# Attention and a mixture of experts on one core: where the next expert's operands are made

## The chip, the cores and the metric

The kernel runs on one core of a Trainium2 chip. TensorE multiplies matrices into PSUM (8 banks of 512 f32 a partition), VectorE (DVE) and ScalarE (ACT) read PSUM and SBUF, GpSimd (POOL) works on SBUF and issues gathers and scatters of rows, SyncE (SP) issues the other DMAs. Each engine executes its own instructions in the order in which they were written. The metric is the time of one execution on the device, in microseconds (us); the median of several runs counts.

## The reference, cut to what matters

Attention over 4 batches, 8 heads, 768 positions gives 3072 rows of 512 numbers, x. Each row goes to two of eight experts:

```
for e in range(8):
    for k in range(2):
        mask = top2[:, k] == e
        h = np.maximum(x[mask] @ w1[e], 0.0)              # 512 -> 1024
        out[mask] += top2_w[mask, k, None] * (h @ w2[e])  # 1024 -> 512
```

Everything is f32. The kernel gets near f32 from f16 matmuls: each operand is split into hi = f16(a) and lo = f16(a - hi), and a product is hi*hi + lo*hi + hi*lo.

## The kernel before, in words

Attention fills the first 140 us and is not touched. Then the experts follow, sorted by size: 816, 832, 816, 800, 784, 768, 768, 768 rows at most. Experts 0 and 1 use a plain product. For experts e = 2 to 7 the product x @ w1 is made of **seven half-size products** instead of eight (as Strassen and Winograd do): x and w1 are cut in quarters, and sums of quarters are operands too. These sums, and the hi and lo parts of all operands, must be made for the next expert while the current one computes.

**The seven stage.** For each of four column groups i = 0 to 3 the products u = 1 to 7 are written by `seven(e, i, u)`; below (i,u) names one. Each is six matmuls (`prod`, line 1338) with half of the rows as columns. (i,1) and (i,2) are accumulated in a bank called b1, (i,3) and (i,5) in b5, (i,4), (i,6), (i,7) in b2; b2 and b5 have two banks each, for even and odd i. b1 is og[:, i % 2]: the two halves of one tile `o` of two banks. After (i,1) ScalarE copies b1 into b2 (line 1357), after (i,5) b5 into SBUF (line 1360); after (i,6) VectorE adds into b5 (line 1362), after (i,7) into c22 (line 1364). Four of the seven, u = 2, 3, 4, 7, end with `hi()` on ScalarE (relu to f16, line 1368) and `lo()` on VectorE (line 1371), which write the hidden rows `hth` and `htl`. TensorE's order: (0,1) (0,5) at the end of the expert before (`seven_head`); (0,2) (0,6); then blocks (i,1) (i,5) (i-1,7) (i,2) (i,6) (i-1,3) (i-1,4) for i = 1 to 3; last (3,7), a part of the first chunk's second product, (3,3), (3,4).

**The second stage.** h @ w2 in chunks of 128 rows, 24 matmuls each (line 1405; line 1402 for the last, shorter chunk of a large expert). A chunk is accumulated in a PSUM tile `pt` (two buffers), `mm2_out` (line 912, VectorE) scales it by the gate and adds the rows read earlier from the output (`prev`, a POOL gather), and POOL scatters the row sum back. Experts with up to 768 rows have 6 chunks, larger ones 7. Ahead of the last chunk stands `seven_head` of the next expert, which needs that expert's w1 part 0 and all its tokens.

**What is woven in.** A plan written by hand puts each preparing step at a **hook**: hook t is called after a certain product (3 to 31) or after a third of a chunk (32 + 3c and on, for chunk c). What a hook calls is written on each engine's queue at that place. The steps for the next expert n:

- `w_load` (lines 731, 735): 512 KB of w1 (parts 0 to 3) or w2 (parts 4 to 7) into one of four buffers `stg`, on SP's queue. `w1_sums` (line 1318): four sums of quarters of 128x256 on POOL, into another `stg` buffer. `w1_hi` (ScalarE, line 1327) and `w1_lo` (VectorE, line 1331): two pieces each, 768 and 1024 columns.
- `w_hi`, `w_lo` (lines 740, 758): the w2 parts of expert e itself, during its seven stage, one operation of 1024 columns each.
- `xs_gather`: two row gathers on POOL (line 90) into one of two buffers `xg`, for token group g: 0 to 2 are full (2 x 128 rows), 3 holds the tail rows over 768 (experts 2, 3 and 4 only). `xs_sums` (lines 1272 to 1274): three VectorE operations. `xs_hi` (ScalarE, line 1291) and `xs_lo` (VectorE, line 1300): four pieces each, two for each of two parts. `xs_turn` (line 1307): transposing DMAs on SP's queue into the operand tiles.

The operand tiles are used again from stages that are over: an even expert's hi parts lie in XTE[0] and its lo parts in XTE[1], an odd one's hi parts in w2 tiles of expert 1 and its lo parts in `xl`. XTE[1] holds expert 1's own tokens, which its plain product (mm1, lines 851 to 860, hooks 0 to 15) reads to its end.

Of the kernel before, what the change touches and what calls it, by code (L numbers as in the profile page):

```python
# [8 lines left out]
F32 = mybir.dt.float32  # L9
F16 = mybir.dt.float16  # L10
# [53 lines left out]
def attn_moe(ctx, tc, qt, kt, vt, wgn, noise, w1, w2, out):  # L64
# [1154 lines left out]
            x.rearrange("p a b -> p (a b)")[:, :n]  # L1219

    def seven_init():
        G["xs"] = [[flat16(XTE[0], 14, 1), flat16(XTE[1], 14, 1)], [None, G["xl"]]]
        G["wp"] = [flat16(WT[i][n], 3584, 0).rearrange("p (l o x) -> p l o x", l=2, o=7)
                   for i in range(2) for n in ("w1h", "w1l")]

# [34 lines left out]
                     in_offset=bass.IndirectOffsetOnAxis(ap=ap, axis=0), bounds_check=N - 1, oob_is_err=False)  # L1260
        XR[n, g] = [x.rearrange("p s c -> p (s c)").bitcast(F32), -(-k // 16) * 16]

    def xs_sums(n, g):
        if (n, g) not in XR:
            return
        x, r = XR[n, g]
        t = [work.tile([P, DC, P], F32, name="xt", bufs=GN).rearrange("p a b -> p (a b)") for i in range(2)]
        XR[n, g] += [t[0], t[1]]
        ta, tb = [z[:r] for z in t]
        x = x[:r]  # L1270
        v = x.rearrange("p (a b c) -> p a b c", a=2, b=2)
        nc.vector.tensor_tensor(ta.rearrange("p (a c) -> p a c", a=2), v[:, 1], v[:, :, 0], op=OP.subtract)
        nc.vector.tensor_tensor(tb[:, :256], x[:, 768:], ta[:, :256], op=OP.subtract)
        nc.vector.tensor_tensor(tb[:, 256:], x[:, 256:512], tb[:, :256], op=OP.subtract)

    def xs_pieces(n, g, part):
        x, r, ta, tb = XR[n, g]
# [3 lines left out]

    XH = {}

    def xs_hi(n, g):
        if (n, g) not in XR:
            return
        for part in range(2):
            r, ps = xs_pieces(n, g, part)
            t = XH[n, g, part, 0] = work.tile([P, DM], F32, name="x", bufs=5).bitcast(F16)
            for c, k, src in ps:  # L1290
                nc.scalar.activation(t[:r, c:c + k], src, AF.Copy)  # L1291

    def xs_lo(n, g):
        if (n, g) not in XR:
            return
        for part in range(2):
            r, ps = xs_pieces(n, g, part)
            t = XH[n, g, part, 1] = work.tile([P, DM], F32, name="x", bufs=5).bitcast(F16)
            for c, k, src in ps:
                nc.vector.tensor_tensor(t[:r, c:c + k], src, XH[n, g, part, 0][:r, c:c + k], op=OP.subtract)  # L1300

    def xs_turn(n, g, lo):
        if (n, g) not in XR:
            return
        for part in range(2):
            r = XR[n, g][1]
            nc.sync.dma_start_transpose(out=xs_part(n, lo, part)[:, :, P * g:P * g + r],
                                        in_=XH[n, g, part, lo][:r, :NS_[part]])

    SS = {}  # L1310

    def w1_sums(n, f):
        t = SS[n, f] = stage.tile([P, SW], F32, name="stg")[:, :1024]
        a21, a11, a12, a22 = [SG[n, f][:, 256 * i:256 * i + 256] for i in range(4)]
        s1, s2, s3, s4 = [t[:, 256 * i:256 * i + 256] for i in range(4)]
        for o, x, y, op in ((s1, a21, a22, OP.add), (s2, s1, a11, OP.subtract), (s3, a11, a21, OP.subtract),
                            (s4, a12, s2, OP.subtract)):
            nc.gpsimd.tensor_tensor(o, x, y, op=op)  # L1318

    def w1_parts(n, f):  # L1320
        w = G["wp"][f]
        return [(s, w[:, 0, o].rearrange("p o x -> p (o x)"), w[:, 1, o].rearrange("p o x -> p (o x)"))
                for s, o in ((SG[n, f][:, 256:], slice(0, 3)), (SS[n, f], slice(3, 7)))]

    def w1_hi(n, f):
        for s, hi, lo in w1_parts(n, f):
            nc.scalar.activation(hi, s, AF.Copy, scale=W1S)

    def w1_lo(n, f):
        for s, hi, lo in w1_parts(n, f):  # L1330
            nc.vector.scalar_tensor_tensor(lo, s, W1S, hi, op0=OP.mult, op1=OP.subtract)  # L1331

    def prod(e, f, a, b, ph, start):
        k, w, h = 0, G["wp"][f], CAPS[e] // 2
# [12 lines left out]

    def seven(e, i, u):
        h = CAPS[e] // 2
        b1, b2, b5 = og[:, i % 2, :h], G["b2"][i % 2][:, :h], G["b5"][i % 2][:, :h]  # L1350
        hh, hl = HT
        f = i + (4 if u in (4, 7) else 0)
        t = slice(0, h) if u in (2, 4) else slice(h + tail(e), 2 * h + tail(e))
        a, b = ((0, 0), (1, 1), (6, 2), (2, 6), (3, 3), (4, 5), (5, 4))[u - 1]
        prod(e, i, a, b, {1: b1, 2: b1, 3: b5, 5: b5}.get(u, b2), u in (1, 5))
        if u == 1:
            nc.scalar.activation(b2, b1, AF.Copy)  # L1357
        elif u == 5:
            G["p5", i] = late[0].tile([P, XW], F32, name="p5", bufs=2)[:, :h]
            nc.scalar.activation(G["p5", i], b5, AF.Copy)  # L1360
        elif u == 6:
            nc.vector.tensor_tensor(b5, b2, G["p5", i], op=OP.add)  # L1362
        elif u == 7:
            nc.vector.tensor_tensor(G["c22"][:, :h], b2, G["p5", i], op=OP.add)
        src = {2: b1, 3: b5, 4: b2, 7: G["c22"][:, :h]}.get(u)

        def hi():
            nc.scalar.activation(hh[:, f, t], src, AF.Relu)  # L1368

        def lo():  # L1370
# [66 lines left out]
    def on(t, f, *a):  # L1437
        plan.setdefault(t, []).append((f, a))
# [2 lines left out]
        for f, a in plan.pop(t, []):  # L1441
            f(*a)

    def plan_w1(n, p, *t):
        for x, f in zip(t, (w_load, w1_sums, w1_hi, w1_lo)):
            on(x, f, n, p)

    def plan_x(n, g, *t):
        on(t[0], xs_gather, n, g)
        on(t[1], xs_sums, n, g)  # L1450
        on(t[2], xs_hi, n, g)
        on(t[2], xs_turn, n, g, 0)
        on(t[3], xs_lo, n, g)
        on(t[4], xs_turn, n, g, 1)

    def plan_late(n):
        plan_x(n, 1, 10, 34, 35, 36, 36)
        plan_x(n, 2, 26, 40, 41, 42, 42)
        plan_x(n, 3, 37, 44, 45, 46, 46)
        for i in range(4):  # L1460
            on((40, 40, 45, 45)[i], w_load, n, 4 + i)

    for e in range(1, E):
        pv = []
# [5 lines left out]
        n = e + 1  # L1470
        if e == 1:
            on(0, tail_ids)
            plan_w1(n, 0, 1, 4, 6, 7)
            plan_w1(n, 1, 3, 7, 9, 10)
            plan_w1(n, 2, 8, 11, 38, 39)
            plan_w1(n, 3, 11, 14, 43, 44)
            plan_x(n, 0, 8, 12, 13, 14, 32)
            plan_late(n)
        else:
            for i, (a, b) in enumerate(((3, 3), (4, 7), (8, 10), (11, 12))):  # L1480
                on(a, w_hi, e, 4 + i)
                on(b, w_lo, e, 4 + i)
            on(36, tail_next, e)
            if n < E:
                plan_w1(n, 0, 5, 9, 14, 17)
                plan_w1(n, 1, 13, 16, 32, 33)
                plan_w1(n, 2, 18, 24, 38, 39)
                plan_w1(n, 3, 34, 37, 43, 44)
                plan_x(n, 0, 6, 21, 22, 24, 25)
                plan_late(n)  # L1490
        for t in (17, 20, 23):
            on(t, prev)
        if e == 1:
# [171 lines left out]
```

## Time and profile before

| | |
|---|---|
| three runs | 691.88, 696.96, 700.48 us; median 696.96 |
| profiled execution | 703.5 us, its span in the trace 701.7 us |
| busy in the span | PE 641.4, DVE 451.7, POOL 321.1, ACT 313.4 us |
| expert 1's plain product | 208 to 242 us |
| seven stages | from 290 (expert 2), 361, 432, 501, 571, 637 us |
| second stages between them | 328 to 361, 399 to 432, 470 to 501, 539 to 571, 609 to 637, 668 to the end |

A row of the trace gives the start of an instruction in us from the span's start, its duration, engine, line, tiles written and read, and in brackets how long its engine sat idle before it and what ended that wait. Runs of like instructions are merged (x6), and consecutive instructions may overlap by some 0.1 to 0.2 us. Idle time counts where it delays the end; here that is the idle time of TensorE, which is busy nearly always.

### The profile page before, as it was taken

To read this page: it belongs to the slowest core of one execution; us is meant where nothing else is said; L and a number is where in the kernel's file an instruction comes from. 1 tells how busy PE (TensorE), PEld (TensorE's weight loads), DVE (VectorE), ACT (ScalarE), POOL (GpSimd) and SP (SyncE) were. 2 spreads that over 40 slices of the span, in tenths; PEclk is the share of its full clock that TensorE was granted. 3 is DMA by queue.
4 is the path that set the end of the run, shared out by engine and by line. 5 is a ranking of instruction groups with operands and counts; after the bars stand their busy time and mean duration, and the time that the engine had idled before them with its cause. 6 is when DMAs were issued, how large, how long until landed. Compare 5 with 4: busy or idle time off the path is not lost.

```text
span 701.7 us, 14247 instructions
## 1 busy us (share of the span) xinstructions
PE 641.4 (91%) x5343; PEld 368.1 (52%) x5343; DVE 451.7 (64%) x927; ACT 313.4 (45%) x688; POOL 321.1 (46%) x517
## 2 busy tenths in 40 slices
PE   8899989899999996888988998899989988999995
PEld 7677877655555542444454445444544444445542
DVE  5758988798863655378737774776377637765411
ACT  4777988731523431354334533453345234524300
POOL 4342242123256662294838483737383529353031
PEclk9999999999999999799999999999999999999998
DMA  9999999546493599347944694469546954692021
GB/s 298 314 301 310 320 276 316 206 149 202 148 208 102 134 167 238 110 126 155 245 144 135 153 243 136 138 153 217 187 129 150 226 162 130 150 276 94 1 88 47
DMA packets 123482, 127.81 MB, mean 182 GB/s; under 512 B 83084, under 2 KB 86484, under 8 KB 123404
## 3 DMA queue, kind: packets, MB, share of 16 engines
q1 hardware_dynamic: 111644, 90.54, 48.8%
q0 software_dynamic: 11760, 36.27, 18.1%
q8 instruction: 44, 0.72, 0.5%
q14 instruction: 34, 0.28, 0.1%
HBM read 82.03 MB, written 25.82 MB: 154 GB/s over the span
## 4 chain that ended last, share of the span: by engine, by line
PE 56%; DVE 13%; DMA 10%; issue 9%; ACT 6%; POOL 4%; SPq 2%; POOLq 0%; DVEq 0%; ACTq 0%
PE pt L1405 16%; PE h L851 9%; PE h L1338 7%; DMA xte<-x 5%; PE pt L902 4%; PE o L1338 4%; DVE htl L1371 3%; PE pt L341 2%; PE h L902 2%; PE s L318 2%; PE o L354 2%; DVE x L1300 2%; DVE w1h L1331 2%; ACT hth L1368 2%; DMA prev<-out_dram,tb 2%
## 5 line engine op out<-in xcount | busy, mean ns | idle before, releaser
L90 POOL DMA_INDIRECT out_dram<-y,tb x48 | 57.7, 1201 | 165.1 <-DVE y L912 147.0
L1318 POOL TENSOR_TENSOR stg<-stg 128x256 f32<-128x256 f32 x96 | 87.3, 929 | 32.5 <-DMA stg<-in_w_dram 18.9
L1405 PEld LDWEIGHTS <-hth 128*128 128x128 f16 x576 | 56.8, 99 | 67.8 <-issue 2.2
L90 POOL DMA_INDIRECT xg<-xd,tb x53 | 57.4, 1083 | 61.3 <-DVE dsc L653 31.4
L912 DVE SCALAR_TENSOR_TENSOR y<-pt,tb,prev 128x512 f32<-128x512 f32 x42 | 31.5, 750 | 83.7 <-PE pt L1405 72.5
L1338 PEld LDWEIGHTS <-w1l 128*128 128x128 f16 x504 | 50.9, 101 | 61.4 <-issue 29.5
L1338 PEld LDWEIGHTS <-w1h 128*128 128x128 f16 x504 | 49.4, 99 | 60.0 <-issue 23.1
L1405 PE MATMUL pt<-w2h,hth 128*128 128x512 f16 x288 | 70.1, 384 | 0.0
L1405 PE MATMUL pt<-w2l,hth 128*128 128x512 f16 x288 | 69.6, 381 | 0.0
L1405 PE MATMUL pt<-w2h,htl 128*128 128x512 f16 x288 | 69.0, 379 | 0.0
L1291 ACT ACTIVATE x<-xt 128x512 f16<-128x512 f32 (+2 forms) x42 | 25.6, 626 | 64.0 <-issue 51.7
L90 POOL DMA_INDIRECT prev<-out_dram,tb x42 | 47.6, 1133 | 12.4 <-issue 9.0
L333 ACT ACTIVATE p<-s,nm 128x120 f32<-128x120 f32 x192 | 51.1, 376 | 0.8
L851 PE MATMUL h<-xte,w1h 128*128 128x384 f16 (+2 forms) x248 | 49.4, 338 | 0.0
L1357 ACT ACTIVATE h<-o 128x384 f32<-128x384 f32 (+3 forms) x24 | 11.6, 482 | 80.7 <-PE o L1338 69.6
L1405 PEld LDWEIGHTS <-htl 128*128 128x128 f16 x288 | 28.2, 98 | 34.0
L1338 PE MATMUL h<-xte,w1h 128*128 128x408 f16 (+2 forms) x180 | 36.1, 344 | 5.0 <-DMA xte<-x 2.6
L1368 ACT ACTIVATE hth<-h 128x384 f16<-128x384 f32 (+3 forms) x48 | 23.9, 498 | 36.9 <-PE h L1338 36.5
L1338 PE MATMUL h<-xte,w1l 128*128 128x408 f16 (+2 forms) x180 | 35.8, 342 | 4.5 <-DVE h L1362 4.5
L857 ACT ACTIVATE hth<-h 128x384 f16<-128x384 f32 (+2 forms) x31 | 15.9, 514 | 47.4 <-PE h L851 47.1
L758 DVE SCALAR_TENSOR_TENSOR w2l<-stg,w2h 128x1024 f16<-128x1024 f32 x28 | 35.4, 1264 | 2.3 <-ACT w2h L740 2.3
L851 PEld LDWEIGHTS <-w1h 128*128 128x128 f16 x256 | 24.7, 98 | 19.5 <-issue 0.8
(286 smaller groups left out, 1314.5 us busy)
## 6 DMA issues: line engine op xcount, KB each, us to landing
stg<-in_w_dram SPq DMA_DIRECT2D x64, 512.0 KB
q<-in_qt_dram SPq DMA_DIRECT2D x24, 256.0 KB
xd<-x SPq DMA_DIRECT2D x24, 256.0 KB
out_dram<-xg SPq DMA_DIRECT2D x8, 768.0 KB
kb<-in_kt_dram SPq DMA_DIRECT2D x6, 768.0 KB
hth<-in_vt_dram SPq DMA_DIRECT2D x12, 260.0 KB
htl<-in_vt_dram SPq DMA_DIRECT2D x16, 195.0 KB
ve<-in_vt_dram SPq DMA_DIRECT2D x12, 260.0 KB
```

Source lines behind the costliest of these rows:

```text
L90: return nc.gpsimd.indirect_dma_start(**kw)
L333: nc.scalar.activation(PE_[t][:, a, hp, :], SC[t][:, a, hp, :], AF.Exp, bias=NM[t][:, 1, a, hp:hp + 1], scale=0.125)
L758: nc.vector.scalar_tensor_tensor(lo, SG[e, i], sc, hi, op0=OP.mult, op1=OP.subtract)
L851: nc.tensor.matmul(ph[:, :n], w1_of(w, wn, c, f), x[:, xo + c, c0:c1], start=(k == 0), stop=(k == 11))
L902: nc.tensor.matmul(py, hx[:, f, c * P:c * P + P], wv[:, f, :], start=st, stop=sp)
L912: nc.vector.scalar_tensor_tensor(y, py[:, :d], gw, pv[:, :d], op0=OP.mult, op1=OP.add)
L1291: nc.scalar.activation(t[:r, c:c + k], src, AF.Copy)
L1318: nc.gpsimd.tensor_tensor(o, x, y, op=op)
L1338: nc.tensor.matmul(ph[:, :h], w[:, la, a, P * j:P * j + P], x[:, j, :h], start=start and k == 0, stop=k == 5, skip_group_check=True)
L1368: nc.scalar.activation(hh[:, f, t], src, AF.Relu)
L1371: nc.vector.scalar_tensor_tensor(hl[:, f, t], src, 0.0, hh[:, f, t], op0=OP.max, op1=OP.subtract)
L1405: nc.tensor.matmul(py, x, wv[:, f, :], start=st, stop=sp, skip_group_check=True)
```

## The change

Four things. The sums of w1 quarters go from POOL to VectorE. The preparing steps are cut into single operations, each with a hook of its own, and the hooks are set anew: the next expert's token groups 0 and 1 are made in the seven stage, group 2, the tail and all four w1 parts in the second stage (for expert 2: groups 0 to 2 and w1 parts 0 and 1 during expert 1's plain product); w2 parts 6 and 7 are loaded at hook 4 of their own expert. For odd i, b1 is a `pt` tile in place of the second half of `o`. XTE[1] and `xl` change roles, so expert 2's lo parts lie in `xl`.

```diff
     def seven_init():
-        G["xs"] = [[flat16(XTE[0], 14, 1), flat16(XTE[1], 14, 1)], [None, G["xl"]]]
+        G["xs"] = [[flat16(XTE[0], 14, 1), G["xl"]], [None, flat16(XTE[1], 14, 1)]]
...
+    def xs_lo(n, g, part, i):
...
+        c, k, src = ps[i]
+        nc.vector.tensor_tensor(XH[n, g, part, 1][:r, c:c + k], src, XH[n, g, part, 0][:r, c:c + k], op=OP.subtract)
+        if i == 1:
+            xs_turn(n, g, part, 1)
...
         for o, x, y, op in ((s1, a21, a22, OP.add), (s2, s1, a11, OP.subtract), (s3, a11, a21, OP.subtract),
                             (s4, a12, s2, OP.subtract)):
-            nc.gpsimd.tensor_tensor(o, x, y, op=op)
+            nc.vector.tensor_tensor(o, x, y, op=op)
...
     def seven(e, i, u):
         h = CAPS[e] // 2
-        b1, b2, b5 = og[:, i % 2, :h], G["b2"][i % 2][:, :h], G["b5"][i % 2][:, :h]
+        if u == 1:
+            G["b1", i] = psum.tile([P, 512], F32, name="pt", bufs=2) if i % 2 else og[:, 0]
+        b1, b2, b5 = G["b1", i][:, :h], G["b2"][i % 2][:, :h], G["b5"][i % 2][:, :h]
...
+    def plan_w1(n, p, t, *u):
+        on(t, w_load, n, p)
+        on(u[0], w1_sums, n, p)
+        for i in range(2):
+            on(u[1 + i], w1_hi, n, p, i)
+        for i in range(2):
+            on(u[3 + i], w1_lo, n, p, i)
+
+    def plan_x(n, g, t, s, h, l):
+        on(t, xs_gather, n, g)
+        for i in range(3):
+            on(s[i], xs_sums, n, g, i)
+        for i in range(2):
+            on(h[i], xs_hi, n, g, i)
         for i in range(4):
-            on((40, 40, 45, 45)[i], w_load, n, 4 + i)
+            on(l[i], xs_lo, n, g, i // 2, i % 2)
...
         if e == 1:
             on(0, tail_ids)
-            plan_w1(n, 0, 1, 4, 6, 7)
-            plan_w1(n, 1, 3, 7, 9, 10)
-            plan_w1(n, 2, 8, 11, 38, 39)
-            plan_w1(n, 3, 11, 14, 43, 44)
-            plan_x(n, 0, 8, 12, 13, 14, 32)
-            plan_late(n)
+            plan_x(n, 0, 0, (3, 3, 3), (4, 4), (5, 5, 5, 5))
+            plan_x(n, 1, 1, (6, 6, 6), (7, 7), (8, 8, 8, 8))
+            plan_w1(n, 0, 1, 9, 9, 10, 10, 10)
+            plan_w1(n, 1, 2, 11, 11, 12, 12, 12)
+            plan_x(n, 2, 7, (13, 13, 13), (14, 14), (15, 15, 15, 15))
+            plan_w1(n, 2, 11, 33, 33, 34, 34, 34)
+            plan_x(n, 3, 12, (35, 35, 35), (36, 36), (37, 37, 37, 37))
+            plan_w1(n, 3, 13, 38, 38, 39, 39, 39)
         else:
-            for i, (a, b) in enumerate(((3, 3), (4, 7), (8, 10), (11, 12))):
+            for i, (a, b) in enumerate(((3, 4), (4, 7), (8, 14), (15, 21))):
                 on(a, w_hi, e, 4 + i)
                 on(b, w_lo, e, 4 + i)
             on(36, tail_next, e)
             if n < E:
-                plan_w1(n, 0, 5, 9, 14, 17)
-                plan_w1(n, 1, 13, 16, 32, 33)
-                plan_w1(n, 2, 18, 24, 38, 39)
-                plan_w1(n, 3, 34, 37, 43, 44)
-                plan_x(n, 0, 6, 21, 22, 24, 25)
-                plan_late(n)
+                plan_x(n, 0, 3, (9, 11, 12), (10, 13), (15, 16, 18, 19))
+                plan_x(n, 1, 5, (22, 23, 25), (24, 27), (28, 29, 29, 31))
+                plan_w1(n, 0, 8, 32, 32, 33, 33, 34)
+                plan_w1(n, 1, 15, 35, 35, 36, 36, 37)
+                plan_x(n, 2, 20, (38, 38, 38), (39, 39), (40, 40, 40, 40))
+                plan_w1(n, 2, 35, 41, 41, 42, 42, 43)
+                plan_x(n, 3, 32, (44, 44, 44), (45, 45), (46, 46, 46, 46))
+                plan_w1(n, 3, 38, 47, 47, 48, 48, 49)
+            if e > 2:
+                on(4, w_load, e, 6)
+                on(4, w_load, e, 7)
+        if n < E:
+            on(44, w_load, n, 4)
+            on(44, w_load, n, 5)
+        if e == 1:
+            on(48, w_load, n, 6)
+            on(48, w_load, n, 7)
```

Before, `plan_w1(n, p, load, sums, hi, lo)` and `plan_x(n, g, gather, sums, hi, lo, turn of lo)` had one hook for each whole step, and `plan_late` had groups 1, 2 and 3 at (10, 34, 35, 36, 36), (26, 40, 41, 42, 42), (37, 44, 45, 46, 46).

## Rows read from the trace of the kernel before

**Rows 1.** The page, costliest groups: busy us, mean ns of one, idle before it.

```profile
L1318 POOL TENSOR_TENSOR stg<-stg 128x256 f32<-128x256 f32 x96 | 87.3, 929 | 32.5 <-DMA stg<-in_w_dram 18.9
```

**Rows 2.** Stretches: length, then each engine's busy time, granted clock, DMA share, GB/s.

```profile
208.00:242.00 34.00, 34.00 (x197) 18.90 (x194) 17.31 (x26) 12.73 (x23) 20.08 (x31) 1.00 0.38 112
432.00:470.00 38.00, 33.27 (x183) 18.02 (x180) 26.77 (x40) 20.15 (x36) 22.42 (x32) 0.96 0.46 129
470.00:501.00 31.00, 31.00 (x183) 15.51 (x181) 16.75 (x25) 7.67 (x12) 16.42 (x26) 1.00 0.98 221
```

**Rows 3.** TensorE's waits, 242 to 702 us: total us, how many, longest.

```profile
PE o L1338 <- DVE htl L1371: 12.9, 11, 2.5
PE o L1338 <- DMA xte<-x: 11.4, 3, 5.9
PE h L1338 <- DVE h L1362: 7.5, 5, 2.1
PE h L1338 <- DVE htl L1371: 4.0, 6, 0.9
PE h L1338 <- DMA xte<-x: 2.6, 1, 2.6
PE o L1338 <- DMA xl<-x: 1.8, 1, 1.8
```

**Rows 4.** TensorE in order of time, expert 4's seven products: start, duration, idle before.

```profile
432.11 1.17 PE L1338 MATMUL o<-xte,w1h 128*128 128x392 f16 x6
...
447.53 2.15 PE L1338 MATMUL h<-xte,w1l 128*128 128x392 f16 x12
452.06 1.84 PE L1338 MATMUL o<-xte,w1l 128*128 128x392 f16 x6 [2.37 <-DVE htl L1371]
453.69 2.17 PE L1338 MATMUL h<-xte,w1l 128*128 128x392 f16 x6
```

**Rows 5.** VectorE in order of time, expert 4, both stages.

```profile
447.92 3.14 DVE L1331 SCALAR_TENSOR_TENSOR w1h<-stg,w1h 128x768 f16<-128x768 f32 x2
...
451.45 0.55 DVE L1371 SCALAR_TENSOR_TENSOR htl<-o,hth 128x392 f16<-128x392 f32 x1
...
452.87 0.68 DVE L1272 TENSOR_TENSOR xt<-xg 128x512 f32<-128x512 f32 x1
453.58 0.42 DVE L1273 TENSOR_TENSOR xt<-xg,xt 128x256 f32<-128x256 f32 x1
...
460.42 1.28 DVE L1300 TENSOR_TENSOR x<-xt,x 128x512 f16<-128x512 f32 x2
...
475.78 0.75 DVE L912 SCALAR_TENSOR_TENSOR y<-pt,tb,prev 128x512 f32<-128x512 f32 x1 [0.60 <-PE pt L1405]
476.45 2.08 DVE L1331 SCALAR_TENSOR_TENSOR w1h<-stg,w1h 128x768 f16<-128x768 f32 x2
480.96 0.75 DVE L912 SCALAR_TENSOR_TENSOR y<-pt,tb,prev 128x512 f32<-128x512 f32 x1 [2.43 <-PE pt L1405]
```

**Rows 6.** POOL in order of time, expert 4's seven products.

```profile
435.62 1.29 POOL L90 DMA_INDIRECT xg<-xd,tb  x1 [0.22 <-issue]
...
447.52 4.80 POOL L1318 TENSOR_TENSOR stg<-stg 128x256 f32<-128x256 f32 x4
```

**Rows 7.** All engines, near 155 and 250 us: two gathers and their first readers.

```profile
153.20 1.01 POOL L90 DMA_INDIRECT xg<-xd,tb  x1 [20.06 <-DVE dsc L653]
...
156.66 0.63 ACT L809 ACTIVATE x<-xg 128x512 f16<-128x512 f32 x1 [2.34 <-DMA xg<-xd,tb]
...
244.46 1.00 POOL L90 DMA_INDIRECT xg<-xd,tb  x1 [0.22 <-issue]
...
255.02 0.63 ACT L1291 ACTIVATE x<-xg 128x512 f16<-128x512 f32 x1 [2.43 <-DMA xg<-xd,tb]
```

**Rows 8.** The chain that ended last, 340 to 360 us: start, us, what.

```profile
350.51 1.68 DVE x L1300 x4
...
352.44 4.47 DMA xl<-x
```

More of the change, by code (lines that the diff above doesn't have):

```diff
@@ L1261, in xs_gather, with xs_sums @@
         XR[n, g] = [x.rearrange("p s c -> p (s c)").bitcast(F32), -(-k // 16) * 16]
-    def xs_sums(n, g):
+    def xs_sums(n, g, k):
         if (n, g) not in XR:
             return
[L1266 to L1270, printed above, removed]
-        v = x.rearrange("p (a b c) -> p a b c", a=2, b=2)
-        nc.vector.tensor_tensor(ta.rearrange("p (a c) -> p a c", a=2), v[:, 1], v[:, :, 0], op=OP.subtract)
-        nc.vector.tensor_tensor(tb[:, :256], x[:, 768:], ta[:, :256], op=OP.subtract)
-        nc.vector.tensor_tensor(tb[:, 256:], x[:, 256:512], tb[:, :256], op=OP.subtract)
+        if k == 0:
+            XR[n, g] += [work.tile([P, DC, P], F32, name="xt", bufs=GN).rearrange("p a b -> p (a b)")
+                         for i in range(2)]
+        x, r, ta, tb = XR[n, g]
+        x, ta, tb = x[:r], ta[:r], tb[:r]
+        v = x.rearrange("p (a b c) -> p a b c", a=2, b=2)
+        if k == 0:
+            nc.vector.tensor_tensor(ta.rearrange("p (a c) -> p a c", a=2), v[:, 1], v[:, :, 0], op=OP.subtract)
+        elif k == 1:
+            nc.vector.tensor_tensor(tb[:, :256], x[:, 768:], ta[:, :256], op=OP.subtract)
+        else:
+            nc.vector.tensor_tensor(tb[:, 256:], x[:, 256:512], tb[:, :256], op=OP.subtract)
     def xs_pieces(n, g, part):
@@ L1282, in attn_moe, with xs_hi, xs_turn @@
     XH = {}
-    def xs_hi(n, g):
+    def xs_hi(n, g, part):
         if (n, g) not in XR:
             return
[L1287 to L1293, printed above, removed]
+        r, ps = xs_pieces(n, g, part)
+        t = XH[n, g, part, 0] = work.tile([P, DM], F32, name="x", bufs=5).bitcast(F16)
+        for c, k, src in ps:
+            nc.scalar.activation(t[:r, c:c + k], src, AF.Copy)
+        xs_turn(n, g, part, 0)
+    def xs_lo(n, g, part, i):
         if (n, g) not in XR:
             return
[L1296 to L1308, printed above, removed]
+        r, ps = xs_pieces(n, g, part)
+        if i == 0:
+            XH[n, g, part, 1] = work.tile([P, DM], F32, name="x", bufs=5).bitcast(F16)
+        c, k, src = ps[i]
+        nc.vector.tensor_tensor(XH[n, g, part, 1][:r, c:c + k], src, XH[n, g, part, 0][:r, c:c + k], op=OP.subtract)
+        if i == 1:
+            xs_turn(n, g, part, 1)
+    def xs_turn(n, g, part, lo):
+        r = XR[n, g][1]
+        nc.sync.dma_start_transpose(out=xs_part(n, lo, part)[:, :, P * g:P * g + r],
+                                    in_=XH[n, g, part, lo][:r, :NS_[part]])
     SS = {}
@@ L1322, in w1_parts, with w1_hi, w1_lo @@
         return [(s, w[:, 0, o].rearrange("p o x -> p (o x)"), w[:, 1, o].rearrange("p o x -> p (o x)"))
[L1323 to L1331, printed above, removed]
+                for s, o in ((SG[n, f][:, 256:], slice(0, 3)), (SS.get((n, f)), slice(3, 7))) if s is not None]
+    def w1_hi(n, f, i):
+        x, hi, lo = w1_parts(n, f)[i]
+        nc.scalar.activation(hi, x, AF.Copy, scale=W1S)
+    def w1_lo(n, f, i):
+        x, hi, lo = w1_parts(n, f)[i]
+        nc.vector.scalar_tensor_tensor(lo, x, W1S, hi, op0=OP.mult, op1=OP.subtract)
     def prod(e, f, a, b, ph, start):
@@ L1442, in hook @@
             f(*a)
[L1444 to L1459, printed above, removed]
+    def plan_w1(n, p, t, *u):
[11 more added lines that the diff above has]
+            on(h[i], xs_hi, n, g, i)
         for i in range(4):
-            on((40, 40, 45, 45)[i], w_load, n, 4 + i)
+            on(l[i], xs_lo, n, g, i // 2, i % 2)
     for e in range(1, E):
```

## The prediction

> **What bounds the kernel now.** I read the page first for what the removed work costs: 87.3 us on POOL [rows 1]. It says nothing of the end yet. The view by stretches does: TensorE is busy nearly always, so only time in which it stands still or runs slowly can be won. From 470 to 501 (a second stage) it is busy all the time, from 432 to 470 (a seven stage) only 33.27 of 38.00 us [rows 2]. The table of who waited for whom, for TensorE alone from 242 us on, splits that idle time: 12.9 us in 11 waits of products into `o` on a VectorE `htl`, 4.0 us in 6 waits of products into `h` on `htl`, 7.5 us in 5 waits on line 1362, and 11.4 + 2.6 + 1.8 us in 5 waits on transposing DMAs [rows 3]. Together 40.2 us; all of it lies at the seven products or at the first two products of an expert, which the change rearranges.
>
> The wait into `o` is the largest. Expert 4 shows the pattern: product (3,1) starts at 452.06 after 2.37 us of idling, when the lo of (2,2), at 451.45 for 0.55 us, has ended [rows 4, 5]. Product (3,1) writes og[:,1]; that lo reads og[:,0]. So it is waiting for the neighbour bank in the same tile, not for its own. The lo was late because two lo operations of a weight piece (447.92, 3.14 us) stood ahead of it on VectorE [rows 5]. Then the clock: this product and the next take 1.84 and 2.17 us where an undisturbed one (432.11) takes 1.17 [rows 4]; the granted clock fell to the 1.2 GHz level. The dip costs 1.84 + 2.17 - 2 x 1.17 = 1.7 us. Five experts have the wait (6 further waits into `o` are about 0.2 us); four of the five stages show a granted clock of 0.96 as [rows 2] does for expert 4, the first shows 1.00.
>
> The wait on line 1362 is of the same kind: (3,7) needs b2 after line 1362 of (3,6) has read it, and that stood behind four lo pieces of token operands, the last pair at 460.42 for 1.28 us [rows 5].
>
> **The change part by part.**
> *Own banks.* Odd i now write b1 into a `pt` tile. Products (1,1) and (3,1) no longer share a tile with the lo of (0,2) and (2,2); their slot was last used by a second-stage chunk whose row sum is long done. Removed: 12.9 us [rows 3] and four dips, 4 x 1.7 = 6.8 us.
> *Dealt singly.* Between two products VectorE now gets one piece (0.42 to 0.68 us, or a w2 lo) instead of 2 to 3 us at a time, and the weight pieces leave the seven stage. Line 1362 of (3,6) has only small pieces ahead. Removed: 7.5 us. The waits into `h` on `htl` are product (2,5) waiting for the lo of (0,3), which stands behind a w2 lo at hook 12; there stands now one sum of 0.42 us. Removed: 4.0 us, but see the gather below.
> *Token operands early, XTE[1] and xl swapped.* Expert 2's lo parts no longer need XTE[1], which expert 1's first product still reads; its three full groups are made during that product. The 11.4 us are two waits at that first boundary (9.5 us) and one at the boundary into expert 4; the other two stand at those into experts 3 and 6, whose last transposes are late. Removed: 11.4 + 2.6 + 1.8 = 15.8 us.
> Sum removed: 12.9 + 6.8 + 7.5 + 4.0 + 15.8 = 47.0 us.
>
> *Weight sums from POOL to VectorE.* The 96 operations leave POOL [rows 1], where nothing on the path to the end depended on their speed except through row gathers behind them. On VectorE the nearest operation is a 128x256 subtraction, 0.42 us; four make 1.75 us a piece, 7.0 us an expert. Something comes back: beside a POOL sum (four took 4.80 us from 447.52) the pair of weight lo operations took 3.14 us, with POOL not summing 2.08 us [rows 5, 6]. VectorE's load per expert: the seven stage has 26.77 us now; two weight pieces leave (3.14 and about 2.1), one token group comes: sums of 0.68, 0.42 and 0.42, and lo pieces of 1.28 for one pair and, by its columns, three quarters of that for the other, 3.8 in all [rows 5], so about 25 us of 33 that remain. The second stage has 16.75; minus 3.8, plus two pieces at 2.1, plus 7.0, makes 24 of 31. Row sums come every 5.2 us (475.78 and 480.96) and take 0.75 [rows 5]; a chunk then holds 1.75 + 2.08 + 0.75 = 4.6 us, so a row sum is late by less than the 4.4 us that two `pt` buffers allow. I cost it at zero; if this cover were gone, see the second rival.
> *Expert 1's first product.* TensorE is busy 34.00 of 34.00 us with VectorE at 17.31 [rows 2]. Added: two more token groups (2 x 3.8) and two weight sums (2 x 1.75), 11 us, to about 28 of 34. Three spare banks of 2 us each cover a lag of 2 us around hooks 8 to 13. I take 0.5 us, between 0 and 2.
> *Queues.* SP issues the same loads and transposes in another order; four transposes and two w2 loads leave the second stage, where the DMA share is 0.98, for the seven stage, where it is 0.46 [rows 2]. POOL only loses work, so row gathers start no later.
>
> *What comes back.* (1) Token group 0 is gathered at hook 3 and summed at hook 9. POOL cannot start it before the scatter of the previous expert: expert 4 has its second half issued at 435.62 for 1.29 us, until 436.91 [rows 6], and nothing ahead of it changes. A gather landed 156.66 - 154.21 = 2.45 us after its issue ended when DMA was quiet [rows 7], so at 439.4. (2,5) is due ten products after 432.11, each about 1.0 us (two take 2.15 less one overlap of 0.17, from 447.53 [rows 4]), so at 442.1. Ahead of it on VectorE stand the three sums, lo of (0,7), line 1362, lo of (1,2) and lo of (0,3): 1.6 + 4 x 0.5 = 3.6 us. So the sums should start at 438.5; they are 0.9 us late, and everything behind them on VectorE with them. Five experts have it: 4.5 us (bounds 0 and 40, first rival).
> (2) Experts 3 and 4 have tail rows whose lo still comes at hook 46, behind the row sum of the fifth chunk. Before, these four took 1.68 us from 350.51 and the transpose another 4.47 [rows 8], while the product starts 5.2 us after that chunk. Each transpose now goes out after its own two pieces: 1.0 us of the 1.8 stays, 2.0 us for both. Experts 6 and 7 have group 2 at hook 40 and start at hook 47, two chunks or 10.4 us for a row sum (0.75), the lo (2.2) and two transposes: 0.5 each, 1.0 us.
> (3) In the block of i = 2 the lo of (1,3) must end before (3,5), 8 products or 7.9 us after the block begins. VectorE starts on it about 1.4 us late, with a w2 lo (1.1, the larger of the 2.08 pair), four lo pieces (2.2) and five of its own operations (5 x 0.55) ahead: 7.5, and small gaps between. I take 0.2 us five times, 1.0 us.
> Back: 4.5 + 2.0 + 1.0 + 1.0 + 0.5 = 9.0 us. Net 47.0 - 9.0 = 38.0 us. The profiled execution took 703.5 us (span 701.7), 6.5 above the median, so it would become 665.5 and the median 696.96 - 38.0 = **659 us**.
>
> **Rivals.**
> *The gather decides, and the kernel becomes slower.* Sums at hook 9 hold VectorE in order, hi pieces at hook 10 hold ScalarE. Each us by which the gather lands later than 2.45 is a us at (2,5), five times. Under a full DMA a gather that ended at 245.46 was used only at 255.02, 9.56 us later [rows 7]. With that, 5 x 8.0 = 40 us come back in place of 4.5, with five dips 8.5 more, so 659 + 35.5 + 8.5 = 703 us; it decides from a landing of about 8.4 us. For it: two more w2 loads are in flight there, and the w2 hi at hook 8 waits for one of them, too. Against: the seven stage has a DMA share of 0.46. A middle case, 4.5 us, gives 659 + 10 + 4 x 1.7 = 676. Beside VectorE's operations POOL's issue may also stretch: by the same 3.14/2.08 as VectorE's pair did, two issues of 1.01 us take 1.0 us more, 664 in all. The Trainium skill states it as a general contention (GPSIMD Engine Reference, 8. Key points): GpSimd shares its SBUF interfaces with VectorE instructions that read two SBUF inputs, which are what the change adds; the rows of the sums agree, and by that rule the result would be those 664 us. Chance of this rival in all 0.17.
> *VectorE fills up.* The sum of 24 of 31 and 25 of 33 us leaves no room for waits on ScalarE's hi. If it is behind by 3 us as a stage begins, each of five stages idles 2.0 us again with a dip: 5 x 3.7 = 18.5, 677 us. Against it: pieces move to where VectorE idles now (2.43 us before the row sum at 480.96 [rows 5]). Chance 0.13.
> *The bank is not what is waited for*, or the `pt` slot brings the same wait: 12.9 + 6.8 us stay, 679 us. The order of 451.45 and 452.06 speaks against it. Chance 0.07.
>
> **How the numbers follow.** Forecast 0.58, its own range 650 to 668; unnamed mishaps 0.05. If nothing came back, 696.96 - 47.0 = 650, and 648 with some unlisted dips gone. The range of 648 to 686 takes in the second and third rival and the first one's middle case; 0.17 stays outside. Faster by over 2% (under 683 us, about what can be told from no change): 0.58 + 0.08 + 0.10 + 0.05 = 0.81. Within 2%: 0.06 + 0.03 + 0.02 of the rivals and 0.02 of the mishaps, 0.13. Slower by over 2% (above 711): 0.06, half of it a gather that lands later still, half mishaps.
>
> **What would show it.** No wait into `o` on `htl` before (3,1) and a granted clock of 1.00 in the seven stages; none before (3,7); the first boundary without a DMA wait; a wait of about 1 us before (2,5) with VectorE's first sum held by the gather; no `pt` wait in the second stages. I am wrong if the seven stages keep over 2 us of idling each, above all at (2,5), or if TensorE stalls during expert 1's first product.

## The result, and the profile after

The changed kernel takes 666.49 us (median of 4 runs, 664.94 to 669.17) against 697.59 us before (4 runs, 691.88 to 700.48): a ratio of 0.957, 95% interval 0.950 to 0.964. The profiled execution took 667.14 us, its span 665.3 us; that of the kernel before lay further above its median (703.5 us), which the part on the prediction comes back to.

TensorE's waits from 242 us to the end, which answer to [rows 3]: total us, how many, longest.

```profile
PE h L1340 <- DVE htl L1375: 15.3, 5, 5.1
```

Six kinds of wait have become one; of 40.2 us, 15.3 are left. The five are product (2,5) of experts 2 to 6, 3.11, 1.99, 2.65, 2.45 and 5.12 us, each waiting for the lo of (0,3). (3,1), (3,7) and the first products of all experts wait for nothing.

The stretches that answer to [rows 2]: expert 1's product, expert 4's seven stage with the two products ahead of it, its second stage, and a short one that is used below. Columns are length, then busy time (instructions) of PE, PEld, DVE, ACT and POOL, granted clock, DMA share, GB/s.

```profile
208.00:242.00 34.00, 34.00 (x194) 18.71 (x192) 24.01 (x45) 17.63 (x33) 13.37 (x24) 1.00 0.77 198
402.00:433.00 31.00, 28.35 (x199) 17.07 (x198) 22.34 (x38) 15.93 (x29) 13.09 (x22) 1.00 0.72 189
433.00:465.00 32.00, 32.00 (x157) 15.21 (x156) 24.43 (x45) 12.38 (x20) 12.11 (x18) 1.00 0.74 186
...
414.16:418.71 4.55, 4.55 (x30) 2.68 (x28) 0.83 (x3) 2.28 (x5) 3.32 (x8) 1.00 0.86 293
```

TensorE is without a gap in the first and the third, though VectorE is busy for 24 us in each; the second lacks 2.65 us. The sums stand on VectorE now, at less than half of POOL's time for one in [rows 1] (the page, groups of instructions: busy us, mean ns of one, idle before):

```profile
L1320 DVE TENSOR_TENSOR stg<-stg 128x256 f32<-128x256 f32 x96 | 36.3, 419 | 0.8
```

All engines around the wait of expert 4, in order of time (start, duration, what, idle before and its releaser):

```profile
409.38 0.84 PE L1340 MATMUL o<-xte,w1h 128*128 128x392 f16 x4
...
412.88 1.28 POOL L90 DMA_INDIRECT xg<-xd,tb  x1 [0.22 <-issue]
...
413.31 0.37 SPq L731 DMA_DIRECT2D stg<-in_w_dram  x1
...
414.56 0.57 DVE L1368 TENSOR_TENSOR rh<-h,p 128x392 f32<-128x392 f32 x1
...
418.71 0.69 DVE L1273 TENSOR_TENSOR xt<-xg 128x512 f32<-128x512 f32 x1 [3.58 <-issue]
...
421.53 1.03 DVE L1375 SCALAR_TENSOR_TENSOR htl<-h,hth 128x392 f16<-128x392 f32 x2
...
422.15 0.82 PE L1340 MATMUL h<-xte,w1h 128*128 128x392 f16 x4 [2.65 <-DVE htl L1375]
```

The second half of the gather ends its issue at 414.16 and is used at 418.71: it landed 4.55 us later, not 2.45 as in [rows 7]. VectorE is free from 415.13 and stands at the first sum for 3.58 us, with the lo operations that (2,5) needs queued behind it. The profile names nothing that ended this wait ("issue"), but in the other four experts it names the gather, as here in expert 5:

```profile
482.90 0.69 DVE L1273 TENSOR_TENSOR xt<-xg 128x512 f32<-128x512 f32 x1 [3.33 <-DMA xg<-xd,tb]
```

The landings there took 5.25, 4.00, 4.19 and 5.26 us. At 413.31 a load of 512 KB (w1 part 0) went out beside the gather.

Idle time is not all. From the start of expert 1's product to the end the same 2404 matmuls keep TensorE busy for 446.30 us before and 435.78 after (stretches again; first before, with a short one that is used below, then after):

```profile
208.12:701.70 493.58, 446.30 (x2404) 228.92 (x2402) 286.04 (x426) 182.38 (x316) 251.42 (x373) 0.97 0.61 151
...
154.21:156.66 2.45, 2.45 (x14) 1.08 (x12) 2.22 (x10) 0.11 (x1) 2.02 (x5) 1.00 0.55 135
```

```profile
206.91:665.30 458.39, 435.78 (x2404) 227.32 (x2402) 301.49 (x522) 183.83 (x316) 173.79 (x277) 0.99 0.63 163
```

That is 10.5 us less of slow products; the granted clock of the stretch rises from 0.97 to 0.99. With the 24.9 us less of waiting it makes 35.4 us; the stretches differ by 35.2 us. The spans differ by 36.4 us: the other 1.2 us lie ahead of expert 1's product, where nothing was changed.

### The profile page after: what moved, and what is told of

It is laid out like the page before. It is cut to its first block, busy times and chain, and to the rows that moved or that the text cites. A ratio compares the mean times of both kernels' runs of the same rounds, so it can differ in the third digit from the quotient of the medians.

```text
span 665.3 us, 14189 instructions
## 1 busy us (share of the span) xinstructions
PE 630.2 (95%) x5343; PEld 365.6 (55%) x5343; DVE 467.8 (70%) x1023; ACT 314.5 (47%) x688; POOL 242.9 (37%) x421
## 4 chain that ended last, share of the span: by engine, by line
PE 51%; issue 18%; POOL 12%; DVE 9%; DMA 6%; ACT 2%; SPq 1%; POOLq 0%; DVEq 0%; ACTq 0%
PE pt L1409 14%; PE h L1340 12%; PE h L851 6%; POOL out_dram L90 6%; POOL prev L90 4%; DMA xg<-xd,tb 3%; PE pt L902 2%; PE h L902 2%; PE o L354 2%; PE pt L341 2%; PE pt L1340 2%; POOL xg L90 2%; PE s L318 2%; PE o L1340 2%; DVE nm L325 1%
## 5 line engine op out<-in xcount | busy, mean ns | idle before, releaser
L90 POOL DMA_INDIRECT out_dram<-y,tb x48 | 67.1, 1399 | 193.7 <-DVE y L912 176.9
L1340 PE MATMUL h<-xte,w1h 128*128 128x384 f16 (+3 forms) x180 | 40.8, 336 | 10.9 <-DVE htl L1375 10.9
L1340 PE MATMUL h<-xte,w1l 128*128 128x384 f16 (+3 forms) x180 | 40.9, 337 | 0.0
L1329 ACT ACTIVATE w1h<-stg 128x768 f16<-128x768 f32 (+1 forms) x24 | 22.7, 944 | 37.7 <-DVE stg L1320 37.7
L1329 ACT ACTIVATE w1l<-stg 128x768 f16<-128x768 f32 (+1 forms) x24 | 22.4, 942 | 32.1 <-DVE stg L1320 32.1
L1320 DVE TENSOR_TENSOR stg<-stg 128x256 f32<-128x256 f32 x96 | 36.3, 419 | 0.8
```

The lines of the kernel that those rows point to most:

```text
L90: return nc.gpsimd.indirect_dma_start(**kw)
L1320: nc.vector.tensor_tensor(o, x, y, op=op)
L1329: nc.scalar.activation(hi, x, AF.Copy, scale=W1S)
L1340: nc.tensor.matmul(ph[:, :h], w[:, la, a, P * j:P * j + P], x[:, j, :h], start=start and k == 0, stop=k == 5, skip_group_check=True)
```

## The experiments

Ratios are to the kernel before, with 95% intervals. "Waits" are TensorE's from 205 us to the end.

**1. What makes (2,5) wait.** Theory: the gather of token group 0, held up by the load beside it. Three variants of the changed kernel.

*Group 0 gathered a stage earlier* (with None, `plan_x` plans no gather).

```diff
+        if n + 1 < E:
+            on(46, xs_gather, n + 1, 0)
...
-                plan_x(n, 0, 3, (9, 11, 12), (10, 13), (15, 16, 18, 19))
+                plan_x(n, 0, None, (9, 11, 12), (10, 13), (15, 16, 18, 19))
```

> The changed kernel with token group 0 gathered at hook 46 of the expert before, not at hook 3. If the late rows alone hold (2,5), its five waits (15.3 us) and the clock dips behind three of them (about 4 us) go: about 647 us, TensorE without a wait of 1 us in the seven stages. Rival: VectorE is full and only its next queue shows: a wait of 1 to 2 us stays at (2,5) or moves to (3,5), 655 to 660 us.

Measured: 646.63 us, ratio 0.928 (0.920 to 0.937), and no wait left. VectorE takes the same first sum of expert 4 with no idle time ahead of it:

```profile
409.77 0.56 DVE L1368 TENSOR_TENSOR rh<-h,p 128x392 f32<-128x392 f32 x1
410.25 0.68 DVE L1273 TENSOR_TENSOR xt<-xg 128x512 f32<-128x512 f32 x1
```

From the start of expert 1's product to the end:

```profile
208.93:646.80 437.87, 430.66 (x2404) 225.78 (x2402) 302.40 (x522) 183.21 (x316) 177.22 (x277) 0.99 0.66 171
```

That is 20.5 us shorter than in the changed kernel: 15.3 us of waits and 5.1 us of slow products behind them (TensorE's busy time falls from 435.78 to 430.66 us). So the gather is the whole of what was left, and VectorE is not full.

*The load later.*

```diff
-                plan_w1(n, 0, 8, 32, 32, 33, 33, 34)
+                plan_w1(n, 0, 14, 32, 32, 33, 33, 34)
```

> The changed kernel with the load of w1 part 0 at hook 14 in place of hook 8. If that load's 512 KB beside the gathered rows make them land 4.0 to 5.2 us after their issue, they land in 2.5 to 3.5 us now, the waits before (2,5) shrink from 3.1 to about 1.5 us on average, and the time is about 656 us. If the gather is that slow by itself, or because of the gathers issued behind it, landing and waits stay and the time is 666 us.

Measured: 652.85 us, ratio 0.939 (0.930 to 0.947); waits 5.7 us in five (1.20, 0.41, 0.45, 0.60, 3.08). Expert 4, all engines:

```profile
408.31 1.29 POOL L90 DMA_INDIRECT xg<-xd,tb  x1 [0.22 <-issue]
...
411.93 0.69 DVE L1273 TENSOR_TENSOR xt<-xg 128x512 f32<-128x512 f32 x1 [1.38 <-DMA xg<-xd,tb]
```

The second half's issue ends at 409.60, so the landing is 2.33 us without the load beside it; in experts 3 and 5 it is 2.42 and 2.35, in experts 2 and 6 still 3.34 and 3.22 us. The gather is issued where it was; moving one load is worth 666.49 - 652.85 = 13.6 us. Of expert 6's 5.12 us 3.08 are left; another load (w2, line 735) was issued ahead of its gather there, at 528.44, and whether that is the reason was not tried. The Trainium skill has the mechanism (DMA: Bandwidth & Descriptors, Issuing engines are not separate DMA queues): transfers started by different engines run on the same 16 DMA engines and interleave; these two landings agree with it.

*The gather behind it later.*

```diff
-                plan_x(n, 1, 5, (22, 23, 25), (24, 27), (28, 29, 29, 31))
+                plan_x(n, 1, 13, (22, 23, 25), (24, 27), (28, 29, 29, 31))
```

> The changed kernel with the gather of token group 1 at hook 13 in place of 5. Theory, group 0's gather lands late because of the 512 KB load that starts beside it: the second gather behind it on POOL has no part in it, the waits before product (2,5) stay at 14 to 16 us in five, 664 to 669 us. Rival, two gathers in flight slow each other: the landing after issue falls from 4.0 to 5.2 us toward 2.5 us, the waits fall below 8 us, 655 to 660 us.

Measured: 668.07 us, ratio 0.955 (0.948 to 0.963), waits 16.1 us in five. But the edit did not do what it was meant to. POOL in order of time, expert 2 (the second row is the gather that was to come later):

```profile
279.37 1.36 POOL L90 DMA_INDIRECT xg<-xd,tb  x1 [0.22 <-issue]
...
281.04 1.00 POOL L90 DMA_INDIRECT xg<-xd,tb  x1 [0.21 <-issue]
```

POOL has nothing else to do between hooks 5 and 13, so it issues group 1 right behind group 0 as before. A hook is a place in a queue, not a time. The variant before this one answers the question all the same: there, too, group 1's gather is issued right behind (at 409.90 in expert 4), and group 0's lands in 2.33 us. The second gather does not hold the first.

**2. b1's own banks.** Alone, on the kernel before, and taken back from the kernel after.

```diff
-        b1, b2, b5 = og[:, i % 2, :h], G["b2"][i % 2][:, :h], G["b5"][i % 2][:, :h]
+        if u == 1:
+            G["b1", i] = psum.tile([P, 512], F32, name="pt", bufs=2) if i % 2 else og[:, 0]
+        b1, b2, b5 = G["b1", i][:, :h], G["b2"][i % 2][:, :h], G["b5"][i % 2][:, :h]
```

> The kernel before with one edit: odd i write b1 into a pt tile. If the shared tile is the whole cause of the waits into o, as the prediction summed it, 12.9 us of waits and 6.8 us of dips go: about 678 us. Rival: the late VectorE queue is the cause and the tile only the place where it shows. Then (3,1) starts early, but (3,5) next to it waits for the lo of (1,3), which in the trace of before ends only 0.4 us after the lo that (3,1) waited for; about 0.6 us an expert is won, 3 to 8 us in all: 689 to 694 us, with waits into h on htl in place of those into o.

Measured: 697.66 us, ratio 1.002 (0.998 to 1.007), above both forecasts. The waits, and then all engines in expert 4 (the place of [rows 4, 5]):

```profile
PE h L1338 <- DVE h L1364: 14.6, 11, 3.0
PE h L1338 <- DVE htl L1373: 14.3, 11, 2.0
PE o L1338 <- DMA xte<-x: 9.1, 4, 3.6
PE o L1338 <- DMA xl<-x: 2.1, 1, 2.1
```

```profile
445.75 3.15 DVE L1331 SCALAR_TENSOR_TENSOR w1h<-stg,w1h 128x768 f16<-128x768 f32 x2
447.36 1.16 PE L1338 MATMUL pt<-xte,w1l 128*128 128x392 f16 x6
...
449.77 1.02 DVE L1373 SCALAR_TENSOR_TENSOR htl<-h,hth 128x392 f16<-128x392 f32 x2
450.37 1.16 PE L1338 MATMUL h<-xte,w1l 128*128 128x392 f16 x6 [1.85 <-DVE htl L1373]
```

(3,1) starts at 447.36 with no wait: the neighbour bank was indeed what it waited for. But VectorE is as late as before, behind the same pair of weight lo operations, and the next product, (3,5), waits 1.85 us for a lo in the same queue. The wait on line 1362 (here 1364) grows from 7.5 to 14.6 us. The time is moved, not won.

> The changed kernel with b1 back in the two halves of o. If the tile alone made the waits, (3,1) waits for the lo of (2,2) again and 12.9 + 6.8 us come back: about 686 us. Rival: with the pieces dealt singly the lo of (2,2) is done before (3,1) is due; only the wait of 0.2 us before (1,1) returns, six times: about 668 us.

Measured: 662.66 us, ratio 0.953 (0.945 to 0.962), beside 0.957 of the kernel after: nothing lost. The gather's five waits show at (2,1) now, a product earlier; the other six, of 0.2 to 0.5 us, at (1,1):

```profile
PE o L1340 <- DVE htl L1373: 13.4, 11, 5.1
```

**3. VectorE's queue in the seven stage.** The kernel before, with the four w1 pieces taken to later hooks (sums, hi, lo at 32, 32, 33; 35, 35, 36; 41, 41, 42; 47, 47, 48) and the w2 loads and lo where the change puts them; nothing else.

```diff
-                plan_w1(n, 0, 5, 9, 14, 17)
-                plan_w1(n, 1, 13, 16, 32, 33)
-                plan_w1(n, 2, 18, 24, 38, 39)
-                plan_w1(n, 3, 34, 37, 43, 44)
+                plan_w1(n, 0, 8, 32, 32, 33)
+                plan_w1(n, 1, 15, 35, 35, 36)
+                plan_w1(n, 2, 35, 41, 41, 42)
+                plan_w1(n, 3, 38, 47, 47, 48)
```

> The kernel before with one part of the change: the four w1 pieces are loaded and made at later hooks (sums at 32, 35, 41, 47, their hi and lo right behind), so that no w1 lo stands on VectorE's queue in a seven stage; as in the changed kernel the lo of the last two w2 parts then comes at hooks 14 and 21 and their loads at hook 4. Sums stay on POOL, token pieces stay in lumps, banks and roles of tiles stay. Theory, VectorE's queue in the seven stage is what the waits into o and on line 1362 come from, and the w1 pieces are its bulk: most of the 12.9 us into o and a part of the 7.5 us on line 1362 go, and the dips behind them (about 6 us), 675 to 685 us; the boundary waits of 15.8 us stay. Rival, single dealing of the token pieces is what counts: waits into o stay above 8 us and the time above 690. Other rival, the second stage overfills without the rest of the change: waits of second-stage chunks for pt on VectorE's row sum appear, and the time stays at 690 to 705 with the seven stages clean.

Measured: 708.52 us, ratio 1.014 (1.006 to 1.022), above the 690 to 705 us of the last rival; the profiled execution took 718.33 us, so its waits are read for their place. The waits on VectorE:

```profile
PE pt L1405 <- DVE y L912: 22.8, 8, 5.4
...
PE h L1338 <- DVE h L1362: 5.9, 5, 1.3
...
PE o L1338 <- DVE htl L1371: 1.1, 6, 0.2
```

The 12.9 us into o are 1.1, with b1 in its old banks and the token pieces still in lumps; the 4.0 us into h are gone. So the weight pieces' places in the seven stage were the cause; the w1 pieces and the lo of the last w2 parts were moved together and not tried apart. The waits of the last rival came as well: second-stage chunks wait for VectorE's row sum. Expert 4, first (3,1), without a wait, then all engines in the second stage, in order of time:

```profile
457.76 1.16 PE L1338 MATMUL o<-xte,w1l 128*128 128x392 f16 x6
...
475.47 1.23 POOL L90 DMA_INDIRECT out_dram<-y,tb  x1 [5.08 <-DVE y L912]
...
478.49 2.92 POOL L1318 TENSOR_TENSOR stg<-stg 128x256 f32<-128x256 f32 x4
...
481.44 1.06 ACT L1327 ACTIVATE w1l<-stg 128x1024 f16<-128x1024 f32 x1 [7.77 <-POOL stg L1318]
...
482.53 1.22 DVE L1331 SCALAR_TENSOR_TENSOR w1l<-stg,w1l 128x1024 f16<-128x1024 f32 x1 [4.96 <-ACT w1l L1327]
...
485.82 1.40 DVE L912 SCALAR_TENSOR_TENSOR y<-pt,tb,prev 128x512 f32<-128x512 f32 x2
...
486.61 1.89 PE L1405 MATMUL pt<-w2h,hth 128*128 128x512 f16 x8 [1.86 <-DVE y L912]
```

It is a ring of queues. The sums stand on POOL behind a scatter that waits 5.08 us for a row sum (line 912); the next row sum stands on VectorE behind token pieces and a lo, which waits for a hi on ScalarE, which waits for the sums. TensorE waits for the row sum.

**4. The sums on VectorE.** Alone on the kernel before:

```diff
-            nc.gpsimd.tensor_tensor(o, x, y, op=op)
+            nc.vector.tensor_tensor(o, x, y, op=op)
```

> The kernel before with one edit: the sums of w1 quarters on VectorE. At the old hooks two of the four pieces fall among the seven products, each 1.75 us more on the queue that holds the lo of (2,2) and line 1362. If load on that queue is what counts, the waits into o and on line 1362 grow by 1 to 3 us an expert: 702 to 712 us. Rival: without POOL's sums VectorE's pieces are faster (3.14 us becomes 2.08) and that outweighs it: 690 to 696 us.

Measured: 717.90 us, ratio 1.024 (1.016 to 1.032): slower, and more so than forecast. The waits into o double, those on line 1362 grow from 7.5 to 13.1 us:

```profile
PE o L1338 <- DVE htl L1371: 27.6, 16, 4.5
PE h L1338 <- DVE h L1362: 13.1, 5, 2.7
```

And back on POOL in the best version (group 0 early):

> The version with the early gather (646.6 us), with the four sums of w1 quarters back on POOL at the same hooks. If the place of the sums is worth nothing by itself, since TensorE has over 4 us to spare for each row sum of the second stage: 645 to 650 us and no wait of TensorE. Rival: the sums held POOL's gathers and stretched VectorE's pieces, so their move paid: waits on row sums or on late w1 pieces appear in the second stages, 655 us or more.

Measured: 648.69 us, ratio 0.927 (0.920 to 0.933), where the same with the sums on VectorE has 0.928 (0.920 to 0.937). With hi and lo of each piece a third of a chunk apart, the ring of part 3 does not show: no wait on line 912, and 2.6 us in four small waits elsewhere. At the old hooks the sums on VectorE cost; at the new ones their place is worth nothing measurable.

**5. Single dealing.** The best version with each token group's sums, hi and lo in lumps at one hook.

```diff
-                plan_x(n, 0, None, (9, 11, 12), (10, 13), (15, 16, 18, 19))
-                plan_x(n, 1, 5, (22, 23, 25), (24, 27), (28, 29, 29, 31))
+                plan_x(n, 0, None, (11, 11, 11), (12, 12), (18, 18, 18, 18))
+                plan_x(n, 1, 5, (23, 23, 23), (24, 24), (29, 29, 29, 29))
```

> The version with the early gather, with the token pieces of the seven stage not dealt singly: each group's three sums at one hook (11, 23), its hi pieces at the next (12, 24), its four lo pieces at one (18, 29). If dealing singly is what removed the waits, lumps of 1.6 and 2.2 us bring waits of 0.5 to 2 us before (2,5), (3,5) or (3,7) back in each of five stages: 652 to 662 us. Rival: taking the w1 pieces out of the seven stage was enough, and lumps of this size fit: 647 us, no wait of 0.5 us.

Measured: 650.35 us, ratio 0.931 (0.925 to 0.938), between the two forecasts; the interval overlaps the best version's (0.920 to 0.937). The waits are

```profile
PE h L1340 <- DVE htl L1375: 4.1, 7, 0.8
```

where the best version has none. Dealing singly removes these 4.1 us of waits; that the time gains by it is not shown. None of them is on line 1362.

**6. The first boundary.** The best version with expert 1's plan and the roles of XTE[1] and xl as before (but for one point: the lo operations of expert 2's group 0 stand at hook 32 with their transposes, not at 14, and read the rows of group 2, so a part of its lo are those of other rows).

> The version with the early gather, with the plan of expert 1 and the roles of XTE[1] and xl as before the change (hook 32 for the first lo parts). If these two carry the term of the first boundary: two waits on transposing DMAs come back there, 9 to 10 us, with a slow clock for the first products, 656 to 660 us. Rival: in the other schedule the same transposes are in time: 647 us.

Measured: 646.98 us, ratio 0.927 (0.920 to 0.934); 0.7 us of waiting at the first boundary. So in the changed kernel the 9.5 us there stay away without the swap and the earlier plan; whether these two alone would have removed them was not tried. Among what still differed from before were the w2 loads of the next expert, at hooks 44 and 48. They alone, on the kernel before:

```diff
-            on((40, 40, 45, 45)[i], w_load, n, 4 + i)
+            on((44, 44, 48, 48)[i], w_load, n, 4 + i)
```

> The kernel before with one number pair changed: the loads of the w2 parts at hooks 44, 44, 48, 48 in place of 40, 40, 45, 45, as in the changed kernel. Theory, the 9.5 us at the first boundary come from transposes of expert 2's tokens that stand behind two w2 loads on SP's queue and share the DMA engines with them: the first boundary's waits fall below 3 us, and those into experts 3, 4 and 6 shrink too; 682 to 690 us in all. Rival, the w2 loads are not what makes the transposes late (their number and order on SP, or the late lo at hook 32, are): the 9.5 us stay within 2 us and the time stays within 1% of the kernel before.

Measured: 693.98 us (10 runs), ratio 0.995 (0.991 to 0.999). SP's queue in order of time and the products at the boundary, first before, then here:

```profile
259.89 2.20 SPq L735 DMA_DIRECT2D stg<-in_w_dram  x2
...
262.19 14.74 SPq L1307 DMA_TRANSPOSE xte<-x  x6
...
277.24 0.85 PE L1338 MATMUL o<-xte,w1h 128*128 128x408 f16 x4 [3.68 <-DMA xte<-x]
278.32 2.56 SPq L1307 DMA_TRANSPOSE xte<-x  x2
283.96 0.84 PE L1338 MATMUL o<-xte,w1h 128*128 128x408 f16 x2 [5.88 <-DMA xte<-x]
```

```profile
262.69 1.09 SPq L735 DMA_DIRECT2D stg<-in_w_dram  x2
263.88 6.17 SPq L1307 DMA_TRANSPOSE xte<-x  x4
...
272.45 0.51 PE L1338 MATMUL o<-xte,w1h 128*128 128x408 f16 x2 [0.37 <-DMA xte<-x]
```

Before, a pair of loads stands ahead of six transposes and a second pair ahead of the last two, which end on SP at 280.88; here one pair stands ahead of the last four, which end at 270.05, and the second pair behind them all. The boundary's 9.5 us are 0.37. Whether the loads' place on SP or their traffic counts more was not separated. Of these 9 us only about 4.6 show in the median, which stays above the theory's 682 to 690 us: the waits into o rose from 12.9 to 14.5 us, and at the later boundaries 5.9 us of waits stand (3.3 of them on `xl`) where 6.3 stood before. So the w2 loads made the first boundary late, not the others.

**7. All together.** The best version with the load at hook 14 and b1 in its old banks.

> The changed kernel with the gather of token group 0 issued at hook 46 of the expert before, the first w1 load at hook 14 in place of 8, and b1 again in the two halves of tile o. If the waits of TensorE are all gone already with the early gather, nothing more is to be won: 644 to 649 us, the same as with the early gather alone, no wait of TensorE between 205 and 640 us above 1 us, and b1 in one tile brings back no wait into o. If the single tile for b1 matters as soon as the gather is out of the way, waits into o of 5 us or more show up and the time is 652 or more.

Measured: 648.13 us, ratio 0.930 (0.923 to 0.936): no better. TensorE waits 1.7 us in six waits. The best version stays the changed kernel with group 0 gathered a stage earlier, 646.63 us.

## Why the prediction was right or wrong

**The time.** 659 us were predicted, 666.49 measured, within the range. Between the profiled executions 36.4 us were won where 38.0 were forecast, but that is luck: the working came near its own sum by errors that cancel. The rest of the miss is the step from that execution to the median: 6.5 us were subtracted as a constant, but before's execution lay 5.9 us above its median and after's 0.65. Before's executions differ among themselves, from 691.25 us with a granted clock of 0.991 to 702.80 us with 0.980. That a longer one has more waits and dips, which the change takes out, would explain the step; it is not shown. Medians: 36.4 - 5.9 + 0.65 = 31.1 us.

**Own banks: wrong.** The row that was read right, (3,1) waiting for the neighbour bank, was taken for the cause. The 12.9 + 6.8 us were put on a step worth nothing (part 2). What the prediction named beside it and gave no part of the sum, the 3.14 us pair ahead of the lo, was the cause, and taking the weight pieces out of the seven stage removed the wait (part 3). The third rival priced the banks as not the thing waited for and expected the wait to stay; the wait went, by another edit of the same change.

**Dealt singly: right in sum, wrong in its split.** The waits on line 1362 and into h on `htl` went. Lumps bring back 4.1 us of waits where 7.5 + 4.0 were credited; for the 4.0 us the moved weight pieces suffice. The 7.5 us on line 1362 seem to hang on where the lumps stand rather than on their size: with lumps at the old hooks 5.9 us stay (part 3), with lumps at new hooks none (part 5), though other things differ between these two runs.

**Token operands early, and the swap: right sum, the cause wrong at the first boundary.** The 9.5 us there go with the place of the w2 loads on SP's queue alone, which the prediction listed under queues and costed at nothing; without the swap and the earlier plan they stay away (part 6). What removed the waits at the other boundaries was not tried by itself; the place of the w2 loads alone did not (part 6).

**The sums at zero: right.** 24 us of 31 were forecast for VectorE in the second stage, 24.43 of 32 measured, and no wait for `pt`. Expert 1's product was to cost 0.5 us and shows no wait.

**The gather: the mechanism right, the size not.** The wait stands where the prediction put it, at (2,5) in five experts, with VectorE's first sum held. The issue ended 4.8 us into the stage, as forecast. The mis-sized term is the landing: 2.45 us assumed, 4.00 to 5.26 measured, on average 4.65. The prediction's own formula, 0.9 us and a us for each us of landing above 2.45, gives 5 x 3.1 = 15.5 us, and 15.3 were measured. This is the middle case of its first rival, priced at 676 us, and by its own sign of being wrong (over 2 us of idling in a seven stage, above all at (2,5)) the forecast failed here in four of the five stages; three of the stages have a granted clock of 0.94 or 0.95, not the 1.00 that was to be seen. The row was taken from a quiet stretch (DMA share 0.55 from 154.21 to 156.66); the stretch in question had 0.86 (414.16 to 418.71), because the change sets a load beside the gather. The prediction named the w2 loads that come there and took the quiet value against its own remark; the load that decided was that of w1 part 0. POOL's issue beside VectorE was named as a further price of 1.0 us an expert. It did not come in four experts: the second half takes 1.28 to 1.36 us, but the same issue took 1.27 to 1.32 in the kernel before (1.29 in [rows 6]). In expert 6 the first half takes 1.83 us, 1.05 before.

The contention that the Trainium skill states (GPSIMD Engine Reference, 8. Key points) may be what shows in the scatters instead: POOL issues one in 1399 ns on average after, in 1201 ns before, and in 1216 ns with the sums back on POOL (part 4). TensorE does not wait for them, and the 664 us worked out by that rule are near the measured time for another reason, the landing.

**Where the errors cancel.** The gather gave back 15.3 us instead of 4.5, and 5.1 us of slow products with it: 15.9 us less won. The terms (2), (3) and expert 1's product, 4.5 us, did not come. The dips were taken from one stage; TensorE's busy time says 10.5 + 5.1 = 15.6 us where 6.8 were put. 38.0 - 15.9 + 4.5 + 8.8 = 35.4 us, beside the 35.2 us won from expert 1's product on.

## What to carry to other kernels

Before a wait is credited to an edit, ask who is late, not which buffer is shared: a bank of its own let one product pass and the next one stood for the same queue. Take a transfer's landing time from a stretch with the DMA share that the changed kernel will have there, and look what the change itself issues beside it; one 512 KB load moved behind a gather won 13.6 us. A hook fixes the order in a queue: moving an instruction past nothing moves nothing, and moving two pairs of loads behind transposes on one queue emptied a boundary of 9.5 us, of which 4.6 us show in the median.

## What the runs showed of the hardware

- At the same place of expert 4's seven stage, a gather of rows landed 2.33 us after its issue, and 4.55 us with a load of 512 KB issued beside it.
- The sum of 128x256 f32 took 419 ns on VectorE and 929 ns on POOL in [rows 1], but where VectorE was idle beside it POOL's four took 2.92 us, 0.73 each.
- Slow products cost over a third of what the waits cost: from before to the best version the waits fell by 40.2 us and TensorE's busy time by 446.30 - 430.66 = 15.6 us, for the same 2404 matmuls.
- POOL's issue of a scatter took 1201 ns on average before, 1399 ns after, and 1216 ns with the sums back on POOL at the same hooks; with the sums on VectorE at the old hooks it took 1181 ns, so the engine of the sums alone does not set it.
